# Dynamic convolution and a squared-ReLU feed-forward network: one PSUM tile per output half, first loads in float32, first softmax rows moved within SBUF, conv tiles at multiples of 8

## The chip, the cores and the metric

The kernel runs on one core of one Trainium2 chip. Its time is the device time of one launch in microseconds; the median of several runs is compared. One further execution is taken by the hardware profiler: its own time and its trace are what the rows below come from.

## The reference

Two stages follow one another. First a causal convolution whose weights are given per position: for each of 8 x 4096 positions and 8 heads, a softmax over 7 taps weights the position and the six before it, per head of 24 channels (192 channels in all). Then a feed-forward network without biases, 192 to 2048 to 192, with a squared ReLU between.

```python
w = np.exp(weight_gen - max); w = w / (w.sum(-1) + 1e-9)      # [8, 4096, 8, 7]
x_unf = x_pad[:, idx, :].reshape(B, S, K, H, 24)              # the 7 rows that end at s
a = np.einsum('bshk,bskhg->bshg', w, x_unf).reshape(-1, 192)  # dynamic convolution
h = np.maximum(a @ w_in, 0.0)                                 # 192 -> 2048
out = (h * h) @ w_out                                         # 2048 -> 192, float32
```

## The kernel before

The 32768 positions are cut into 64 blocks of 512 (`TB`), 8 to a batch entry. Products run in float16 with float32 sums. The instructions of each engine run in the order in which the program writes them, and each of the queues (SP's and GpSimd's DMA issues among them) is in order too: what waits at its head holds what stands behind it. The framework puts in the waits between engines, by tile: a writer of a tile waits for its readers and the other way round; a buffer of a pool is given out again when the last user of its tile is done.

Softmax. `Softmax` (L118) handles a stretch of rows: `load` (L123) brings the raw weights from DRAM by SP's queue, `exp` (L146) runs on ScalarE, `recip` (L158) and `scale` (L167) on VectorE, and the result goes to a tile `v` with r rows to a partition, in a layout with zero padding between taps. `store` (L185) writes it to a DRAM buffer `vd`. The first batch entry is cut into three parts of 8, 8 and 16 rows to a partition (`FIRST`, tiles `v_first`); each later one is one part of 32, which `plan` (L413) spreads over some of the blocks ahead of it.

Convolution. A block is covered by 5 overlapping tiles of 128 input rows (`starts`, step `STEP`), which yield the output ranges between `bounds`. `x_load` (L221) brings the x rows by GpSimd's queue and casts float32 to float16 on the way; `wr_load` (L225) brings the softmax rows from `vd` by SP's queue. `st_band` (L231) multiplies them with a band mask on VectorE and so makes a banded matrix `bd` for each tile; its slice of the mask begins at `shifts`. `st_conv` (L272) multiplies x with the bands in 72 matmuls of 32 or fewer output columns, in which a piece of the lower and one of the upper 256 positions run side by side in the array; `conv_pieces` (L252) pairs them. `st_y_evac` (L290) copies the result to SBUF as float16 `y`.

Feed-forward. `st_mm1` (L297) computes 2 of 16 chunks of the hidden layer into a PSUM tile `h`; lower and upper positions use the two halves of the array's rows, so `w_i` holds w_in twice, in partitions 0 to 63 and 64 to 127. `st_relu` (L331) runs on ScalarE into `t1` (pool `p_t1`), `st_sq` (L336) on VectorE into `g`. `st_mm2` (L313) adds the chunks up in `o`, one tile of two PSUM banks, half 0 of the positions in one and half 1 in the other. `o_copy` (L342) copies a half to SBUF on ScalarE, `o_store` writes it out. The three buffers of `ps_h` serve `h` and the conv's result `yp`; `ps_o` has one buffer.

The loop (L430). Block j runs conv(j+1) and the copy of its y, bands 0 to 2 of block j+2, the first product for four pairs of chunks (`G0`) with relu and square, then the second product of block j-1 for the chunks `G1`: half 0, its copy, half 1, its copy, and the store. Then bands, a part of a softmax, the first product for `G1` and the second product of block j for `G0`. At the end `wr_load(j+3)`. Blocks 0 and 2 are `late`: their bands come at the end. For j = 0 conv(1) stands in the middle of the block.

The start (L368 to L410). 48 matmuls on zeros warm TensorE up. x of block 0, w_in (four quarters) and w_out go by GpSimd's queue with the cast; w_in is copied to the upper partitions by SP's queue. The first two softmax parts are computed and stored to `vd`, and `wr_load(0)` and `wr_load(1)` read them from there. Then come the bands, the conv and the copy of y of block 0.

Of the kernel before, what the change touches and what calls it, by code (L numbers as in the profile page):

```python
# [9 lines left out]
def kernel(  # L10
# [47 lines left out]
    STEP = 98  # L58
    BASE = -8
    starts = [BASE + STEP * i for i in range(NT)]  # L60
    bounds = [0, 104, 208, 304, 400, TB]
# [7 lines left out]
    p_wg = ctx.enter_context(tc.tile_pool(name="p_wg", bufs=2))  # L69
    p_sm = ctx.enter_context(tc.tile_pool(name="p_sm", bufs=2))  # L70
# [4 lines left out]
    p_t1 = ctx.enter_context(tc.tile_pool(name="p_t1", bufs=6))  # L75
# [25 lines left out]

    WQ = 4

    def load_w_in():
        src = moe_w_in.rearrange("(k p) f -> p k f", p=RT)
        for q in range(WQ):
            c = slice(q * Dff // WQ, (q + 1) * Dff // WQ)
            nc.gpsimd.dma_start(out=w_i[0:RT, :, c], in_=src[:, :, c])

    def copy_w_in(q):  # L110
        c = slice(q * Dff // WQ, (q + 1) * Dff // WQ)
        nc.sync.dma_start(out=w_i[RT:P, :, c], in_=w_i[0:RT, :, c])

    def load_w_out():
        nc.gpsimd.dma_start(out=w_o, in_=moe_w_out.rearrange("(c p) m -> p c m", p=P))


    class Softmax:  # L118
# [27 lines left out]
        def exp(self, lo, hi):  # L146

            if lo == 0:
                self.ex = p_wg.tile([P, self.rh, HP, KK, 2], f32, name=f"ex{self.r}")
                self.ssum = p_sm.tile([P, self.rh, HP, 2], f32, name=f"ssum{self.r}")  # L150
                self.rcp = p_sm.tile([P, self.rh, HP, 2], f32, name=f"rcp{self.r}")
            nc.scalar.activation(  # L152
                out=self.ex[:, lo:hi].rearrange("p r g k e -> p (r g) k e"),
                in_=self.wg[:, lo:hi].rearrange("p r (g e) k -> p (r g) k e", e=2),
                func=ActF.Exp,
            )
# [67 lines left out]

    def wr_load(j):  # L225
        wr_t[j] = p_wr.tile([P, NT, HP, SL * 2], f16, name="wr")
        block_load(
            j, wr_t[j].rearrange("p t g c -> p t (g c)"), vd_t[j // NBB], H * SL, nc.sync
        )

# [82 lines left out]
    def st_mm2(j, fps, halves=(0, 1)):  # L313

        if fps[0] == 0:
            o_t[j] = ps_o.tile([P, 2, TB], f32, name="o")
        o = o_t[j]
        for fp in fps:
            for jj in range(2):
                fc = 2 * fp + jj  # L320
                for half in halves:
                    for cc in range(2):
                        nc.tensor.matmul(  # L323
                            out=o[:, half, cc * Dm : (cc + 1) * Dm],
                            lhsT=g_t[(j, fp)][:, half, jj, cc * P : (cc + 1) * P],
                            rhs=w_o[:, fc, :],
                            start=(fc == 0 and cc == 0), stop=(fc == NF - 1),
                            skip_group_check=True,
                        )
# [12 lines left out]
    def o_copy(j, half, copy):  # L342
        if half == 0:
            o_sb_t[j] = p_os.tile([P, 2, 2 * Dm], f32, name="o_sb")
        copy(out=o_sb_t[j][:, half], in_=o_t[j][:, half, 0 : 2 * Dm])  # L345
# [20 lines left out]
    with nc.allow_low_precision("fp16 matmul pipeline"), tc.manual_schedule():  # L366
# [7 lines left out]
        for i in (0, 1):  # L374
            parts[i].load(nc.sync)
            nc.vector.memset(v_first[i], 0.0)

        wp = ps_h.tile([P, 2 * TB], f32, name="wp", tag="h")
        for i in range(48):
            nc.tensor.matmul(  # L380
                out=wp[:, 0:TB], lhsT=warm[:, 0:P], rhs=warm, start=True, stop=True
            )
        x_load(0)
        load_w_in()
        band_mask()

        for i in (0, 1):
            s = parts[i]
            s.exp(0, s.rh)
            s.recip(0, s.rh)  # L390
            s.scale(0, s.rh, nc.vector)
            s.store(nc.sync)
            if i == 0:
                wr_load(0)
                wr_load(1)
                copy_w_in(0)
                copy_w_in(1)
        copy_w_in(2)
        copy_w_in(3)
        parts[2].load(nc.sync)  # L400
        x_load(1)
        load_w_out()
# [4 lines left out]
        nc.gpsimd.memset(v_first[2], 0.0)  # L407
        nc.gpsimd.memset(v_big, 0.0)
        x_load(2)
        wr_load(2)  # L410
# [19 lines left out]
        for j in range(NBLK):  # L430
# [9 lines left out]
            late = j in (0, 2)  # L440
            if j:
                if j + 1 < NBLK:
                    st_conv_alloc(j + 1)
                    st_conv(j + 1)
                    st_y_evac(j + 1)
                if not late:
                    st_bands(j + 2, BANDS[0:3])
            else:
                st_bands(1, BANDS[0:3])
# [9 lines left out]
            elif NBLK > 1:  # L459
                st_bands(1, BANDS[3:5])  # L460
                st_conv_alloc(1)
                st_conv(1)
                st_y_evac(1)
            if not late:
                st_bands(j + 2, BANDS[3:5])
            if hi:
                s = rows_of[nb]
                s.exp(lo, hi)
                s.recip(lo, hi)
                s.scale(lo, hi, nc.vector)  # L470
# [6 lines left out]
            st_mm2(j, G0)  # L477
            if late:
                st_bands(j + 2, BANDS)
# [38 lines left out]
```

## Time and profile before

| | us |
|---|---|
| median of 3 runs (865.69 to 867.62) | 865.83 |
| profiled execution | 863.74 |
| its span, from the first to the last instruction | 862.0 |
| TensorE, ScalarE, VectorE, GpSimd busy | 789.4, 604.4, 592.2, 69.4 |

The profile names the engines PE (TensorE), PEld (its weight loads), DVE (VectorE), ACT (ScalarE), POOL (GpSimd) and SP (the engine that only issues DMAs); SPq and POOLq are DMA issues. A line of the timeline gives the start, the busy time and the operation with its output and inputs, and in brackets how long the engine was idle before it and what ended that. The granted clock is a share of 2.4 GHz: 1.00 is that level and 0.50 is 1.2 GHz.

### The profile page before, as it was taken

The page shows a single profiled execution, that of the slowest core. Times are in us where ns is not written, and L with a number is a line of the kernel's source. Part 1 is how long each engine was busy: PE and PEld are TensorE (multiplying, and loading weights), DVE is VectorE, ACT ScalarE, POOL GpSimd, SP SyncE. Part 2 cuts the span into 40 slices and gives each one's busy share as a digit, 9 for nine tenths or more (in the row PEclk, how much of TensorE's full clock was granted, in tenths as well). Part 3 has the DMA queues.
Part 4 walks back from the last instruction along what each step waited for, and adds up shares of the span by engine and source line. Part 5 has one row for each costly group of instructions (what it writes and reads, how often), then busy time and mean ns, then how long its engine had stood idle before and what let it go on. Part 6 is the DMA issues. An engine that isn't in the chain of part 4 may idle for free.

```text
span 862.0 us, 32753 instructions
## 1 busy us (share of the span) xinstructions
PE 789.4 (92%) x14896; PEld 682.2 (79%) x14896; DVE 592.2 (69%) x1159; ACT 604.4 (70%) x753; POOL 69.4 (8%) x86
## 2 busy tenths in 40 slices
PE   6898999999999999999999999999999999999997
PEld 3577788888888888888888888888888888878886
DVE  5668777776776767777677767767767766656643
ACT  1575777777777767767767767777677677677674
POOL 6100000000001000010000000000000000000000
PEclk9799999999999999999999999999999999999999
DMA  9632532335433443335333353333533234232111
GB/s 182 143 77 40 142 49 59 69 47 134 69 47 60 88 103 59 68 48 136 66 47 62 66 122 64 63 48 68 134 53 65 58 58 83 58 64 42 46 39 37
DMA packets 124906, 63.85 MB, mean 74 GB/s; under 512 B 87777, under 2 KB 122464, under 8 KB 124000
## 3 DMA queue, kind: packets, MB, share of 16 engines
q0 software_dynamic: 45008, 17.31, 18.6%
q1 hardware_dynamic: 79488, 44.26, 18.3%
q8 instruction: 116, 1.90, 0.9%
q10 hardware_dynamic: 272, 0.20, 0.1%
q14 instruction: 22, 0.18, 0.1%
HBM read 48.90 MB, written 29.36 MB: 91 GB/s over the span
## 4 chain that ended last, share of the span: by engine, by line
PE 62%; issue 16%; ACT 16%; DVE 3%; DMA 2%; ACTq 0%; SPq 0%; DVEq 0%
PE o L323 31%; PE h L304 26%; ACT t L334 12%; PE yp L280 6%; ACT o_sb L345 3%; DVE bd L239 1%; DMA wr<-vd 1%; DVE g L340 1%; DMA vd<-v_first 1%; ACT ex L152 0%; DVE ssum L160 0%; DVE v_first L173 0%; DVE rcp L165 0%; DMA wg<-in_weight_gen_dram 0%; DVE v_big L173 0%
## 5 line engine op out<-in xcount | busy, mean ns | idle before, releaser
L334 ACT ACTIVATE t<-h 128x1024 f16<-128x1024 f32 x512 | 483.0, 1029 | 10.0 <-PE h L304 9.5
L340 DVE TENSOR_TENSOR g<-t 128x1024 f16<-128x1024 f16 x512 | 346.2, 690 | 190.4 <-ACT t L334 190.1
L323 PE MATMUL o<-w_o,g 128*128 128x192 f16 x4096 | 370.3, 246 | 53.8 <-ACT o_sb L345 53.8
L323 PEld LDWEIGHTS <-g 128*128 128x128 f16 x4096 | 332.3, 98 | 90.0 <-issue 71.9
L304 PE MATMUL h<-y,w_i 64*128 64x256 f16 x6144 | 364.6, 271 | 1.4 <-ACT y L293 0.9
L304 PEld LDWEIGHTS <-w_i 64*128 64x128 f16 x6144 | 292.9, 95 | 53.2 <-issue 11.5
L239 DVE TENSOR_TENSOR bd<-wr,mask 128x832 f16<-128x832 f16 (+2 forms) x320 | 168.7, 579 | 10.1 <-DMA wr<-vd 10.0
L293 ACT CAST y<-yp 128x768 f16<-128x768 f32 x64 | 51.1, 799 | 137.6 <-PE yp L280 137.6
L345 ACT COPY o_sb<-o 128x384 f32<-128x384 f32 x127 | 62.8, 494 | 101.0 <-PE o L323 101.0
L219 POOL DMA_DIRECT2D xt<-in_x_dram x56 | 48.3, 862 | 621.6 <-PE yp L280 596.3
L280 PE MATMUL yp<-bd,xt 128*32 128x104 f16 (+14 forms) x4608 | 63.8, 203 | 12.2 <-DVE bd L239 11.8
L280 PEld LDWEIGHTS <-xt 128*32 128x32 f16 (+3 forms) x4608 | 52.1, 91 | 24.5 <-issue 24.5
L160 DVE TENSOR_REDUCE ssum<-ex 128x64 f32<-128x448 f32 (+6 forms) x49 | 25.9, 530 | 57.7 <-ACT ex L152 57.7
L173 DVE TENSOR_TENSOR v_big<-ex,rcp 128x112 f16<-128x112 f32 (+3 forms) x192 | 32.8, 235 | 1.6
L152 ACT ACTIVATE ex<-wg 128x448 f32<-128x448 f32 (+6 forms) x49 | 26.4, 539 | 2.6 <-DMA wg<-in_weight_gen_dram 2.6
L165 DVE RECIPROCAL rcp<-ssum 128x64 f32<-128x64 f32 (+6 forms) x49 | 23.3, 476 | 1.7
L380 PE MATMUL wp<-warm 128*128 128x512 f16 x48 | 12.0, 417 | 1.3 <-DVE warm L373 1.3
L211 POOL DMA_DIRECT2D xt<-in_x_dram x8 | 4.6, 573 | 88.8 <-PE yp L280 88.0
L380 PEld LDWEIGHTS <-warm 128*128 128x128 f16 x48 | 5.0, 106 | 7.8 <-issue 1.9
L173 DVE TENSOR_TENSOR v_first<-ex,rcp 128x112 f16<-128x112 f32 (+2 forms) x32 | 6.3, 269 | 0.2
L217 POOL DMA_DIRECT2D xt<-in_x_dram x8 | 6.0, 749 | 0.5 <-issue 0.5
L345 DVE COPY o_sb<-o 128x384 f32<-128x384 f32 x1 | 0.6, 559 | 3.6 <-PE o L323 3.6
(14 smaller groups left out, 14.1 us busy)
## 6 DMA issues: line engine op xcount, KB each, us to landing
out_dram<-o_sb SPq DMA_DIRECT2D x63, 384.0 KB, 2.7
xt<-in_x_dram POOLq DMA_DIRECT2D x56, 240.0 KB, 4.1
wg<-in_weight_gen_dram SPq DMA_DIRECT2D x6, 1064.0 KB, 6.7
wr<-vd SPq DMA_DIRECT2D x56, 80.0 KB, 2.9
vd<-v_big SPq DMA_DIRECT2D x7, 512.0 KB, 2.9
xt<-in_x_dram POOLq DMA_DIRECT2D x8, 192.0 KB, 3.8
wg<-in_weight_gen_dram SPq DMA_DIRECT2D x1, 896.0 KB, 5.3
wg<-in_weight_gen_dram SPq DMA_DIRECT2D x2, 392.0 KB, 3.2
```

The lines of the kernel that those rows point to most:

```text
L152: nc.scalar.activation(out=self.ex[:, lo:hi].rearrange("p r g k e -> p (r g) k e"), in_=self.wg[:, lo:hi].rearrange("p r (g e) k -> p (r g ...
L160: nc.vector.tensor_reduce(out=ssum.rearrange("p r g e -> p (r g) e"), in_=self.ex[:, lo:hi].rearrange("p r g k e -> p (r g) e k"), axis=Ax ...
L173: eng.tensor_tensor(out=bass.AP(tensor=v.tensor, offset=v.offset + lo * H * SL + lo % SL * 2 + g * SL * 2, ap=[list(v.ap[0]), [H * SL + 2, ...
L219: eng.dma_start(out=dst, in_=rows(src, t0 + BASE, width))
L239: nc.vector.tensor_tensor(out=bd_t[j][:, H * lo : H * hi].rearrange("p (g m c) -> p g m c", g=HP, c=2 * SL), in0=wr_t[j][:, i].unsqueeze(2 ...
L280: nc.tensor.matmul(out=yp_t[j][p0 : p0 + m, col + a : col + b], lhsT=x_t[j][:, i, 32 * q : 32 * q + m], rhs=bd[:, h // 2, h % 2, a - lo : ...
L293: nc.scalar.copy(out=y, in_=yp_t[j][:, 0 : NK * TH].rearrange("p (k c) -> p k c", k=NK))
L304: nc.tensor.matmul(out=h[:, half, jj, :], lhsT=w_i[r0 : r0 + RT, k, fc * P : (fc + 1) * P], rhs=y_t[j][r0 : r0 + RT, k, :], start=(jj == 0 ...
L323: nc.tensor.matmul(out=o[:, half, cc * Dm : (cc + 1) * Dm], lhsT=g_t[(j, fp)][:, half, jj, cc * P : (cc + 1) * P], rhs=w_o[:, fc, :], star ...
L334: nc.scalar.activation(out=t1, in_=h_t[(j, fp)], func=ActF.Relu)
L340: nc.vector.tensor_tensor(out=g, in0=t1, in1=t1, op=AluOp.mult)
L345: copy(out=o_sb_t[j][:, half], in_=o_t[j][:, half, 0 : 2 * Dm])
```

## The change

The output tile `o` becomes two tiles, `o0` and `o1`, one for each half. The start loads x of blocks 0 and 1, w_in and w_out as float32 by SP's queue into staging tiles (pool `p_st`, two buffers of each kind; w_in is loaded twice, once for each half of the partitions), and ScalarE (x, two quarters of w_in) or GpSimd (the other two quarters, w_out) casts them. The softmax rows of blocks 0 and 1 are moved from `v_first[0]` to `wr` within SBUF, five DMAs a block, and the stores to `vd` stand later in SP's queue. For these moves tile starts have to be multiples of 8, so the step of the conv tiles becomes 104, their base -32, and two of the bounds move. `p_t1` has 5 buffers instead of 6, `ex` its own pool. In block 0 the bands of block 1 stand ahead of the loop, those of block 2 in its middle, and its part of the softmax moves to the end. There are 52 warm-up matmuls.

```diff
-    STEP = 98
-    BASE = -8
+    STEP = 104
+    BASE = -32
-    bounds = [0, 104, 208, 304, 400, TB]
+    bounds = [0, 96, 200, 304, 400, TB]
...
+    p_ex = ctx.enter_context(tc.tile_pool(name="p_ex", bufs=2))
+    p_st = ctx.enter_context(tc.tile_pool(name="p_st", bufs=2))
-    p_t1 = ctx.enter_context(tc.tile_pool(name="p_t1", bufs=6))
+    p_t1 = ctx.enter_context(tc.tile_pool(name="p_t1", bufs=5))
...
-    def load_w_in():
+    def load_w_in(q):
         src = moe_w_in.rearrange("(k p) f -> p k f", p=RT)
-        for q in range(WQ):
-            c = slice(q * Dff // WQ, (q + 1) * Dff // WQ)
-            nc.gpsimd.dma_start(out=w_i[0:RT, :, c], in_=src[:, :, c])
-
-    def copy_w_in(q):
         c = slice(q * Dff // WQ, (q + 1) * Dff // WQ)
-        nc.sync.dma_start(out=w_i[RT:P, :, c], in_=w_i[0:RT, :, c])
-
-    def load_w_out():
-        nc.gpsimd.dma_start(out=w_o, in_=moe_w_out.rearrange("(c p) m -> p c m", p=P))
+        w_st[q] = p_st.tile([P, NK, Dff // WQ], f32, name="w_st")
+        for r0 in (0, RT):
+            nc.sync.dma_start(out=w_st[q][r0 : r0 + RT], in_=src[:, :, c])
+
+    def cast_w_in(q, copy):
+        c = slice(q * Dff // WQ, (q + 1) * Dff // WQ)
+        copy(out=w_i[:, :, c], in_=w_st[q])
+
+    def load_w_out(q):
+        n = NF // WO
+        wo_st[q] = p_st.tile([P, n, Dm], f32, name="wo_st")
+        nc.sync.dma_start(
+            out=wo_st[q],
+            in_=moe_w_out[q * n * P : (q + 1) * n * P].rearrange("(c p) m -> p c m", p=P),
+        )
+
+    def cast_w_out(q, copy):
+        n = NF // WO
+        copy(out=w_o[:, q * n : (q + 1) * n], in_=wo_st[q])
...
+    def x_load_f32(j):
+        x_st[j] = p_st.tile([P, NT, D], f32, name="x_st")
+        block_load(j, x_st[j], x[j // NBB], D, nc.sync)
+
+    def x_cast(j, copy):
+        x_t[j] = p_x.tile([P, NT, D], f16, name="xt")
+        copy(out=x_t[j], in_=x_st[j])
...
+    def wr_load_sbuf(j, s):
+
+        wr_t[j] = p_wr.tile([P, NT, HP, SL * 2], f16, name="wr")
+        for i in range(NT):
+            t0 = j * TB + (0 if i == 0 and j == 0 else starts[i]) - s.t0
+            nc.sync.dma_start(
+                out=wr_t[j][:, i].rearrange("p g c -> p (g c)"),
+                in_=s.v[t0 // s.r : (t0 + P) // s.r, HALO : HALO + s.r].rearrange(
+                    "p r g c e -> p r (g c e)"
+                ),
+            )
...
-            o_t[j] = ps_o.tile([P, 2, TB], f32, name="o")
+            o_t[j] = [ps_o.tile([P, TB], f32, name=f"o{half}") for half in range(2)]
...
-                            out=o[:, half, cc * Dm : (cc + 1) * Dm],
+                            out=o[half][:, cc * Dm : (cc + 1) * Dm],
...
-        copy(out=o_sb_t[j][:, half], in_=o_t[j][:, half, 0 : 2 * Dm])
+        copy(out=o_sb_t[j][:, half], in_=o_t[j][half][:, 0 : 2 * Dm])
...
-        for i in range(48):
+        for i in range(52):
...
-        x_load(0)
-        load_w_in()
         band_mask()
...
+        nc.gpsimd.memset(v_first[2], 0.0)
+        nc.gpsimd.memset(v_big, 0.0)
+        vec, act, pool = nc.vector.tensor_copy, nc.scalar.copy, nc.gpsimd.tensor_copy
...
+        parts[0].load(nc.sync)
+        x_load_f32(0)
+        parts[1].load(nc.sync)
+        load_w_in(0)
+        load_w_in(1)
+        s0, s1 = parts[:2]
+        s0.exp(0, s0.rh)
+        s1.exp(0, s1.rh)
+        s0.recip(0, s0.rh)
+        s0.scale(0, s0.rh, nc.vector)
+        wr_load_sbuf(0, s0)
+        x_cast(0, act)
+        x_load_f32(1)
+        cast_w_in(0, act)
+        cast_w_in(1, act)
+        load_w_in(2)
+        s1.recip(0, s1.rh)
+        s1.scale(0, s1.rh, nc.vector)
+        wr_load_sbuf(1, s0)
+        load_w_in(3)
+        for q in range(WO):
+            load_w_out(q)
+            if q == 0:
+                s0.store(nc.sync)
+                s1.store(nc.sync)
+                wr_load(2)
+                for i in (2, 3):
+                    cast_w_in(i, pool)
+            cast_w_out(q, pool)
         parts[2].load(nc.sync)
-        x_load(1)
-        load_w_out()
         st_bands(0, BANDS)
         st_conv_alloc(0)
         st_conv(0)
         st_y_evac(0)
-        nc.gpsimd.memset(v_first[2], 0.0)
-        nc.gpsimd.memset(v_big, 0.0)
+        x_cast(1, act)
+        st_bands(1, BANDS)
         x_load(2)
-        wr_load(2)
...
-            late = j in (0, 2)
+            late = j == 2
...
-            else:
-                st_bands(1, BANDS[0:3])
...
-                st_bands(1, BANDS[3:5])
                 st_conv_alloc(1)
                 st_conv(1)
                 st_y_evac(1)
+                st_bands(2, BANDS[0:3])
...
-            if hi:
+            if hi and j:
...
             st_mm2(j, G0)
+            if hi and not j:
+                softmax(rows_of[nb], lo, hi)
```

## Rows read from the trace of the kernel before

**Rows 1.** Page, part 1: busy us, share of the span, instructions of each engine.

```profile
PE 789.4 (92%) x14896; PEld 682.2 (79%) x14896; DVE 592.2 (69%) x1159; ACT 604.4 (70%) x753; POOL 69.4 (8%) x86
```

**Rows 2.** List of waits: engine line <- releaser, total us, times, longest us.

```profile
PE o L323 <- ACT o_sb L345: 53.8, 64, 0.8
```

**Rows 3.** Timeline of block 20: start, busy us, engine, line, operation, [idle before].

```profile
290.11 0.94 PE L280 MATMUL yp<-bd,xt 128*32 128x104 f16 x72
...
290.98 2.79 PE L304 MATMUL h<-y,w_i 64*128 64x256 f16 x48
...
293.71 1.49 PE L323 MATMUL o<-w_o,g 128*128 128x192 f16 x16
...
296.05 1.48 PE L323 MATMUL o<-w_o,g 128*128 128x192 f16 x16 [0.84 <-ACT o_sb L345]
...
297.46 2.79 PE L304 MATMUL h<-y,w_i 64*128 64x256 f16 x48
297.56 0.48 ACT L345 COPY o_sb<-o 128x384 f32<-128x384 f32 x1 [1.57 <-PE o L323]
...
298.28 0.27 DVE L160 TENSOR_REDUCE ssum<-ex 128x16 f32<-128x112 f32 x1 [0.93 <-ACT ex L152]
...
300.19 2.81 PE L323 MATMUL o<-w_o,g 128*128 128x192 f16 x32
...
302.93 0.94 PE L280 MATMUL yp<-bd,xt 128*32 128x104 f16 x72
```

**Rows 4.** Timeline of block 2, the one with 16 softmax rows.

```profile
62.65 3.76 ACT L334 ACTIVATE t<-h 128x1024 f16<-128x1024 f32 x4
...
63.72 0.83 PE L304 MATMUL h<-y,w_i 64*128 64x256 f16 x12 [0.35 <-ACT t L334]
...
66.45 2.49 DVE L340 TENSOR_TENSOR g<-t 128x1024 f16<-128x1024 f16 x4
```

**Rows 5.** Timeline of the tail.

```profile
856.58 1.48 PE L323 MATMUL o<-w_o,g 128*128 128x192 f16 x16 [0.57 <-ACT o_sb L345]
```

**Rows 6.** Timeline of the start.

```profile
5.61 2.61 POOL L97 TENSOR_SCALAR_AFFINE_SELECT mask<-mask 128x256 f16<-128x256 f16 x2
...
6.86 2.23 DVE L173 TENSOR_TENSOR v_first<-ex,rcp 128x112 f16<-128x112 f32 x8
...
10.89 1.46 DVE L173 TENSOR_TENSOR v_first<-ex,rcp 128x112 f16<-128x112 f32 x8
11.79 2.47 POOL L408 MEMSET v_big<- 128x2816 f16 x1
...
22.74 5.63 PE L304 MATMUL h<-y,w_i 64*128 64x256 f16 x48 [0.89 <-ACT y L293]
...
41.73 2.79 PE L304 MATMUL h<-y,w_i 64*128 64x256 f16 x48
```

**Rows 7.** Chain of work that ended last, 0 to 60 us: start, us, what.

```profile
9.11 4.75 DMA vd<-v_first
...
13.88 4.51 DMA wr<-vd
```

**Rows 8.** Windows: stretch, us, busy of each engine, granted clock, DMA share, GB/s.

```profile
17.00:19.00 2.00, 0.00 (x0) 0.00 (x0) 0.51 (x2) 0.00 (x0) 0.00 (x0) 0.75 1.62 193
19.00:21.00 2.00, 1.48 (x50) 1.11 (x50) 2.00 (x5) 0.00 (x0) 0.00 (x0) 0.50 1.53 235
...
300.00:301.00 1.00, 1.00 (x16) 0.82 (x11) 0.77 (x2) 1.00 (x2) 0.00 (x0) 1.00 1.08 385
```

**Rows 9.** Page, part 6: DMA issues, count, KB each, median us to landing.

```profile
xt<-in_x_dram POOLq DMA_DIRECT2D x56, 240.0 KB, 4.1
...
wr<-vd SPq DMA_DIRECT2D x56, 80.0 KB, 2.9
...
wg<-in_weight_gen_dram SPq DMA_DIRECT2D x2, 392.0 KB, 3.2
```

**Rows 10.** DMA queues view, issues: count, KB each, median us to landing.

```profile
vd<-v_first SPq DMA_DIRECT2D x1, 256.0 KB, 2.0
```

## What the change does to the time, predicted from these rows

> **What bounds the kernel now.** I read the page's busy times first, then the list of waits, then one block of the main loop line by line, then the two ends of the span. TensorE is busy 92% of the span, ScalarE 70%, VectorE 69% [rows 1]: TensorE is the engine to look at, so the question is what stands in its remaining 8%. The list of waits answers it: of TensorE's idle time 53.8 us, in 64 pieces of at most 0.8 us, is its second product waiting for ScalarE's copy of the output [rows 2]. The block shows where. The block's conv starts at 290.11, the next one's at 302.93, so a block is 12.82 us. Inside, TensorE runs without a hole except at one place: the 16 matmuls of output half 0 start at 293.71 and take 1.49 us, and the 16 matmuls of half 1 start only at 296.05, behind an idle time of 0.84 us that ended with that copy [rows 3]. Half 1 needs nothing of that copy; both halves are parts of one tile `o`, and the wait is on the tile.
>
> **Change 1, an output tile per half.** The same work without the wait stands in the same block: the other 32 matmuls of the second product start at 300.19 and are done at 302.93, 2.74 us; those of the halves take from 293.71 to 297.46, 3.75 us [rows 3]. The difference, 1.01 us, is the wait plus the emptying and refilling of the pipeline around it; the idle time alone would be 53.8 / 64 = 0.84. I take 1.01, since it compares start with start, and keep 0.84 as the poor end. 63 blocks give 63 x 1.01 = 63.6 us. In the tail half 1 starts at 856.58, after 0.57 us of the same wait [rows 5]: 0.6 us more. Together 64.2 us (53.8 at the poor end).
>
> What is late next? After the change half 1 starts at once and everything behind it moves up by 1.0 us. ScalarE waits 1.57 us for half 1 before it copies it, which becomes 0.57: it still waits for TensorE and not TensorE for it. VectorE's row sum of the softmax waits 0.93 us for the exponential [rows 3]; that goes to about zero and VectorE stays on time. Loads per block are 604.4 / 64 = 9.4 us for ScalarE and 592.2 / 64 = 9.3 us for VectorE [rows 1], against a new block of 11.81 us, so neither becomes the bound. The accumulator's next use, the first half of the second product at 300.19, comes 2 us after the copies even when all move up together, so the two new tiles with one buffer each cost no wait. They take the same two banks.
>
> **Change 2, `p_t1` with 5 buffers in place of 6.** It would cost something where ScalarE runs five relus ahead of VectorE's squares. The worst place is the block with 16 softmax rows: four relus start from 62.65 and the first of their squares at 66.45 [rows 4], so four are open. Five hold them: nothing, and a slip of one more relu would still only shift ScalarE. `p_ex` renames a pool: nothing.
>
> **Change 3, conv tiles.** The widths of the band tiles are the same set (96, 96, 104, 104, 112), so VectorE pays the same. On TensorE the pieces of the two halves run side by side: the longer of each pair were 104, 104, 112 columns (320), now 96, 104, 112 (312). The conv's 0.87 us (290.11 to 290.98) [rows 3] would shrink by 8/320, 0.02 us, or 1.4 us over 64 blocks; if it is bound by issuing 72 instructions, nothing. I take 0.7.
>
> **Change 4, the start.** I count to the first matmul of block 1's first product, at 41.73 us, from which the kernel runs evenly; block 0's starts at 22.74 [rows 6]. Before it stands a detour through DRAM: the store of the first softmax rows takes 4.75 us and their reload 4.51 [rows 7]. Now five moves within SBUF replace both. None is in the trace; bounds are the 2.9 us of a steady `wr` load [rows 9] and that 4.51. With five issues of about 0.45 us behind one another the tile is complete some 4.5 to 6 us after the rows, in place of 9.3, if the queue is free. It isn't quite: SP now carries two softmax loads, x and two quarters of w_in, 2.9 MB, before the moves. At the 385 GB/s that the queues reached in the steady part [rows 8] it is done at about 9.2 us, level with the rows; at two thirds of that at 13. Block 0's first product then starts at 17.5 to 20 us, a gain of 3 to 5 us.
>
> But that is not what block 1 starts on. `x_load(2)` stays on GpSimd's queue, and GpSimd now first casts two quarters of w_in and four of w_out, 2 x 1536 + 4 x 768 = 6144 elements of a partition; before, nothing but memsets and the mask stood there. conv(2) opens block 1 and needs that x. The chain, each step from a row or a neighbour of it: SP has issued the two stores at about 17.5; they land 2.0 us later as the third store did [rows 10], or 4.75 as the first [rows 7]; `wr_load(2)` waits for them, and `load_w_out(1)` stands behind it, issued at about 22; 3 us to land, as the 392 KB loads (3.2) [rows 9], and 1 us to cast (26); `load_w_out(3)` may use the staging buffer only then: 3 us and 1 us (30.5); x in 4.1 us [rows 9] (34.6); conv and the copy of y, 0.9 + 0.8. Block 1's first product starts at about 36.5 to 37: 4.8 us earlier than 41.73.
>
> From that the clock takes something back. With no matmul to run since the warm-up, TensorE's granted clock fell from 2.4 to 1.2 GHz (0.75 as the mean of 17 to 19 us, 0.50 after) [rows 8], and the first product of block 0 then took 5.63 us, against 2.79 us in block 1 [rows 6]. By the chain TensorE is idle from about 29 to 34.6, so block 1 opens slowly: 2.8 us lost. Net 2 us gained. The four extra warm-up matmuls end about 1 us later than before, ahead of the bands: nothing.
>
> Bounds: with stores that land in 2 us and no fall of the clock the gain is 8 us. The casts have no row; GpSimd's nearest are the memset, 2816 elements in 2.47 us (0.88 ns each), and the mask's select, two of 256 elements in 2.61 us (5.1 ns each) [rows 6]. A cast is a plain stream like the memset, with a read added: I take 1.3 ns, 8 us in all, mostly under the loads. At 5.1 ns it is 31 us, and from about 16 us on they would hold x until 51: a loss of 11 + 2.8 = 14 us. ScalarE's casts lie ahead of conv(0) and are covered by the wait for the moves.
>
> Sum: 862.0 - 64.2 - 0.7 - 2.0 = 795.1 us of span. The profiled execution took 863.74, 1.74 more than its span, and the median of the runs is 865.83, another 2.09 more: 798.9, rounded to 799.
>
> **Rivals.**
> (a) GpSimd's casts are slow. Eight scalings with two operands took 2.23 us while GpSimd ran the select, and 1.46 us while it only wrote a memset [rows 6]; so the two engines do hold each other up. The casts read, and VectorE's bands, squares and scalings have two operands: some 9.3 us of them in a block [rows 1], all of which may delay the casts in front of x, to 808. Slower casts give up to 815.6. The Trainium skill, "SBUF — State Buffer", section "Who interferes with whom", says that a VectorE instruction with two SBUF inputs contends with a GpSimd instruction that reads SBUF and not with one that only writes; the 2.23 against 1.46 us agrees.
> (b) Another wait takes the place of the one removed. One is in sight: where the exponential is long, the fourth tile of the next product waited 0.35 us for ScalarE's relu [rows 4]. That chain starts at the copy of half 1 and moves with it, which speaks against it. If each block paid it, 22 us come back: 821.
> (c) The split doesn't remove the wait, because the order and not the shared tile makes it. Against it: half 1's operands were ready and the release is the copy's. 862.0 - 0.7 - 2.0 + 3.83 = 863.1, no change.
> (d) Slower than before: the casts on GpSimd hold x(2) and w_out for so long that the start eats all 66.9 us. Each ns per element costs 6.1 us, so it decides from 1.3 + 11 = 12 ns on, at twice the slowest row; 18 ns would give 900.
>
> **Chances.** The forecast 0.72; (a) 0.16; (b) 0.06; (c) 0.04; (d) 0.02. The forecast's own ends are 862.0 - 64.2 - 1.4 - 8 + 3.83 = 792.2 and, with 0.84 us per block, 809.3; (a) reaches 815.6. I say 790 to 815. A difference of 0.3% is about what a measurement of this kernel can tell: faster 0.94, same 0.04, slower 0.02.
>
> **What would show it.** Right: no wait of the second product for `o_sb` in the list, a block of 11.8 us from conv to conv, ScalarE's wait before the copy of half 1 down to about 0.6 us, block 1's first product at 36 to 37 us, TensorE idle before conv(2) with x as the releaser. Wrong: a new idle time of TensorE inside the block, a conv(2) that waits for something else, casts on GpSimd of more than 2 ns per element, or a clock that falls outside the start.

## The result, and the profile after

The kernel takes 806.39 us after the change (median of 4 runs, 803.74 to 810.45) and 865.76 us before, beside it on the same chip: a ratio of 0.932, with a 95% interval of 0.9274 to 0.936. The profiled execution took 806.78 us with a span of 804.9. The forecast was 799.0, in a range of 790 to 815. The main loop gained what was forecast; the start lost where a gain was forecast.

The page of the changed kernel, part 1, answers to [rows 1]:

```profile
PE 779.5 (97%) x14900; PEld 682.0 (85%) x14900; DVE 592.9 (74%) x1159; ACT 609.8 (76%) x757; POOL 70.3 (9%) x84
```

TensorE's busy time is down by 9.9 us, 9.5 of them in the second product (370.3 to 360.8 us); the rest of the 57.1 us of span was idle time. Its list of waits answers to [rows 2] (engine line <- releaser: total us, times, longest):

```profile
PE yp L315 <- DMA xt<-in_x_dram: 8.7, 1, 8.7
PE yp L315 <- DVE bd L274: 6.1, 6, 2.9
PE o L358 <- POOL w_o L130: 2.4, 1, 2.4
PE h L339 <- POOL w_i L118: 1.5, 1, 1.5
...
PE h L339 <- ACT t L369: 0.3, 1, 0.3
```

The 53.8 us for `o_sb` are gone, and no wait that recurs in every block has come. What is left stands at the start, with one new wait of 8.7 us for an x. The timeline of one block, which answers to [rows 3] (start, busy us, engine, line, operation):

```profile
255.32 0.92 PE L315 MATMUL yp<-bd,xt 128*32 128x96 f16 x72
256.17 2.79 PE L339 MATMUL h<-y,w_i 64*128 64x256 f16 x48
258.89 2.81 PE L358 MATMUL o<-w_o,g 128*128 128x192 f16 x32
261.64 2.79 PE L339 MATMUL h<-y,w_i 64*128 64x256 f16 x48
264.37 2.81 PE L358 MATMUL o<-w_o,g 128*128 128x192 f16 x32
267.11 0.68 PE L315 MATMUL yp<-bd,xt 128*32 128x96 f16 x48
...
261.74 0.48 ACT L380 COPY o_sb<-o 128x384 f32<-128x384 f32 x1 [0.56 <-PE o L358]
```

The two halves are one group of 32 matmuls without a hole, and from conv to conv a block is 267.11 - 255.32 = 11.79 us. ScalarE still waits for half 1, 0.56 us in place of 1.57. The tail answers to [rows 5] in the same way:

```profile
795.68 5.45 PE L358 MATMUL o<-w_o,g 128*128 128x192 f16 x64
```

One row on each side divides the time: block 2's first product, of before and then of after.

```profile
54.75 1.48 PE L304 MATMUL h<-y,w_i 64*128 64x256 f16 x24
```

```profile
60.26 1.48 PE L339 MATMUL h<-y,w_i 64*128 64x256 f16 x24
```

From there to the end of the span it is 862.0 - 54.75 = 807.3 us before and 804.9 - 60.26 = 744.6 after: 62.6 us gained. Up to there 5.5 us are lost. The lost time is in these rows of the start, timeline first, then the chain of waits (start, us, what):

```profile
17.38 0.22 PE L315 MATMUL yp<-bd,xt 128*32 128x96 f16 x2 [2.88 <-DVE bd L274]
...
21.02 4.97 PE L339 MATMUL h<-y,w_i 64*128 64x256 f16 x48 [0.89 <-ACT y L328]
...
45.77 1.48 PE L315 MATMUL yp<-bd,xt 128*32 128x96 f16 x72 [8.73 <-DMA xt<-in_x_dram]
47.18 3.86 PE L339 MATMUL h<-y,w_i 64*128 64x256 f16 x48
...
8.56 4.12 SPq L259 DMA_DIRECT2D wr<-v_first  x5
```

```profile
4.83 11.64 DMA w_st<-in_moe_w_in_dram
...
17.15 4.89 DMA wr<-v_first
...
23.79 5.78 DMA vd<-v_first
...
30.05 3.75 DMA wo_st<-in_moe_w_out_dram
...
39.17 6.56 DMA xt<-in_x_dram
```

Block 1's first product comes at 47.18, where it came at 41.73 before [rows 6]: the x of conv(2) was asked for at 39.17 and landed at 45.73, and TensorE stood idle for 8.73 us. The same links as in the forecast's chain are there, in the same order; each is later, and each transfer takes longer.

### The profile page after: what moved, and what is told of

It reads as the page before. It is cut to its first block, busy times and chain, and to the rows that moved or that the text cites. A ratio compares the mean times of both kernels' runs of the same rounds, so it can differ in the third digit from the quotient of the medians.

```text
span 804.9 us, 32787 instructions
## 1 busy us (share of the span) xinstructions
PE 779.5 (97%) x14900; PEld 682.0 (85%) x14900; DVE 592.9 (74%) x1159; ACT 609.8 (76%) x757; POOL 70.3 (9%) x84
## 4 chain that ended last, share of the span: by engine, by line
PE 92%; DMA 4%; DVE 1%; SPq 1%; issue 1%; POOL 0%; ACT 0%; DVEq 0%; POOLq 0%
PE o L358 43%; PE h L339 43%; PE yp L315 7%; DMA w_st<-in_moe_w_in_dram 1%; DMA xt<-in_x_dram 1%; DMA vd<-v_first 1%; DMA wr<-v_first 1%; DVE bd L274 1%; DMA wo_st<-in_moe_w_out_dram 0%; POOL w_o L130 0%; SPq L114 0%; DVE g L375 0%; DVE v_big L188 0%; ACT ex L167 0%; DVE ssum L175 0%
## 5 line engine op out<-in xcount | busy, mean ns | idle before, releaser
L358 PE MATMUL o<-w_o,g 128*128 128x192 f16 x4096 | 360.8, 247 | 2.4 <-POOL w_o L130 2.4
L274 DVE TENSOR_TENSOR bd<-wr,mask 128x768 f16<-128x768 f16 (+2 forms) x320 | 170.0, 583 | 12.5 <-DMA wr<-vd 7.6
L234 POOL DMA_DIRECT2D xt<-in_x_dram x55 | 47.5, 864 | 554.0 <-PE yp L315 519.4
L315 PE MATMUL yp<-bd,xt 128*32 128x96 f16 (+17 forms) x4608 | 61.7, 203 | 15.1 <-DMA xt<-in_x_dram 8.7
L226 POOL DMA_DIRECT2D xt<-in_x_dram x7 | 3.9, 559 | 80.9 <-PE yp L315 80.9
L232 POOL DMA_DIRECT2D xt<-in_x_dram x7 | 5.2, 748 | 0.0
L118 ACT CAST w_i<-w_st 128x1536 f16<-128x1536 f32 x2 | 2.9, 1472 | 2.9 <-DMA w_st<-in_moe_w_in_dram 2.9
```

Source lines behind the costliest of these rows:

```text
L234: eng.dma_start(out=dst, in_=rows(src, t0 + BASE, width))
L274: nc.vector.tensor_tensor(out=bd_t[j][:, H * lo : H * hi].rearrange("p (g m c) -> p g m c", g=HP, c=2 * SL), in0=wr_t[j][:, i].unsqueeze(2 ...
L315: nc.tensor.matmul(out=yp_t[j][p0 : p0 + m, col + a : col + b], lhsT=x_t[j][:, i, 32 * q : 32 * q + m], rhs=bd[:, h // 2, h % 2, a - lo : ...
L358: nc.tensor.matmul(out=o[half][:, cc * Dm : (cc + 1) * Dm], lhsT=g_t[(j, fp)][:, half, jj, cc * P : (cc + 1) * P], rhs=w_o[:, fc, :], star ...
```

## The experiments

**The split alone, and the change without it.** Two kernels divide the change: before with nothing but a tile per half (e1), and after with one tile `o` again (e2).

```diff
-            o_t[j] = ps_o.tile([P, 2, TB], f32, name="o")
+            o_t[j] = [ps_o.tile([P, TB], f32, name=f"o{half}") for half in range(2)]
...
-        copy(out=o_sb_t[j][:, half], in_=o_t[j][:, half, 0 : 2 * Dm])
+        copy(out=o_sb_t[j][:, half], in_=o_t[j][half][:, 0 : 2 * Dm])
```

> The kernel before with one edit: an output tile per half; loads, softmax moves and conv tiles stay as they were. Theory: the wait for the shared tile is worth 1.0 us in each of 63 blocks and 0.6 in the tail, 64 us, and the changed start gave some 5 of them back. Then this kernel is faster than the changed one: 865.8 - 64 = 802 us, block 1's first product still at 41.7 us, the block 11.8 us. Rival 1: the start is neutral and the split is worth only the 59 us that were measured: 806. Rival 2: the shorter block hangs on the conv tiles too: block over 11.9 us and 810 or more.

Measured: 802.59 us, ratio 0.9277 (0.926 to 0.9295).

> The changed kernel with one edit undone: one output tile for both halves again. Theory: everything else in the change costs 5 us at the start and gains 1 us in the conv; with the wait back the block is 12.8 us and the time 806.4 + 64 = 870, slower than the kernel before by 4 to 5 us, with block 1's first product at 47 us. Rival: the rest of the change is neutral or gains, and the time is 866 or less.

Measured: 869.76 us, ratio 1.005 (1.0032 to 1.0068). The list of waits of e2 has the old row again:

```profile
PE o L358 <- ACT o_sb L380: 53.3, 64, 0.8
```

So the split is worth 62 to 63 us, all of the gain and more; the rest of the change costs 4 to 5 us, whichever way it is taken.

**Is it the shared tile, or the copy between the halves?** e3 keeps one tile and moves the order: both halves' matmuls first, then both copies.

```diff
             for half in (0, 1):
                 st_mm2(j - 1, G1, (half,))
+            for half in (0, 1):
                 o_copy(j - 1, half, nc.scalar.copy)
```

> The kernel before with one edit: both halves of the second product first, then both copies; still one output tile. Theory: half 1 waits because the tile has a reader between its writers; with the readers behind both, TensorE's wait for the copy goes as with two tiles (64 us), but ScalarE now has two copies to make before its first relu of the next product, 0.4 to 0.5 us later than with the split, so the fourth tile of that product waits for the relu 0.1 us in blocks without softmax and 0.4 us in blocks with: 802 + 0.3 x 63 = 815 to 825 us, new waits of TensorE for the relu in nearly each block. Rival: ScalarE's delay is hidden and it is as fast as the split, 802. Rival 2: the wait isn't the tile's, and 0.84 us of idle time stays in front of half 1: 866.

Measured: 817.03 us, ratio 0.9439 (0.9417 to 0.9462). TensorE's and the weight loads' waits of e3, then the weight loads' of e1:

```profile
PE h L304 <- ACT t L334: 7.5, 22, 0.7
...
PEld L304 <- issue: 28.3, 114, 0.9
```

```profile
PEld L304 <- issue: 12.3, 71, 0.6
```

The 53.8 us go away here too, so the wait hung on a copy standing between two groups of matmuls on one tile. But ScalarE now does both copies after the second half, its relus start later, and TensorE waits for them in the blocks that carry a part of a softmax: these take 11.98 to 12.30 us from conv to conv in e3's steady part and 11.82 to 11.92 in e1's, the blocks without one 11.82 in both. 14 us come back. The two tiles remove the wait and leave ScalarE its early start.

**What the start waits for.** e4 changes one place of the changed kernel: x of block 2 is asked for behind GpSimd's two casts of w_in, ahead of those of w_out.

```diff
                 for i in (2, 3):
                     cast_w_in(i, pool)
+                x_load(2)
...
         x_cast(1, act)
         st_bands(1, BANDS)
-        x_load(2)
```

> The changed kernel with one move: GpSimd loads x of block 2 behind its two casts of w_in, ahead of the four casts of w_out. Theory: conv(2) waited 8.7 us for this x; without that it is ready when the second product of block 0 ends, and what is late next is the third softmax load, which holds ScalarE's queue until about 40 us: block 1's first product at 41 to 42 us in place of 47.2, TensorE still idle in front of it and its clock down: 806.4 - 5.5 = 801. Rival: x comes no earlier, as the DMA queues are full with the weights until then, and the time stays at 806.

Measured: 800.31 us, ratio 0.9249 (0.9234 to 0.9264), 6 us under the changed kernel: the place of `x_load(2)` behind the casts was the last link. What is late next in e4, by its chain of waits:

```profile
21.99 5.98 DMA vd<-v_first
...
28.45 5.97 DMA wo_st<-in_moe_w_out_dram
...
36.28 4.58 DMA wg<-in_weight_gen_dram
```

conv(2) runs at 38.54, and then its y waits behind an exponential on ScalarE whose weights landed at 40.9: the same queue of SyncE, one link further. Block 2's first product is at 53.42.

Three kernels ask what holds that queue. e5 reorders it, puts two w_out loads and a w_g load on ScalarE's queue, and issues the ten moves of softmax rows one behind the other. e8 moves only block 0's rows within SBUF and sends block 1's through DRAM; it also issues the first two w_out loads and the third softmax load earlier, as e5 does, but on SyncE's queue. e9 sends all of them through DRAM, as before the change. The cores of the three edits, each against e4, in this order:

```diff
         wr_load_sbuf(0, s0)
         x_cast(0, act)
-        x_load_f32(1)
...
-        load_w_in(2)
...
         wr_load_sbuf(1, s0)
+        s0.store(nc.sync)
+        x_load_f32(1)
+        load_w_in(2)
+        s1.store(nc.sync)
...
+        load_w_out(0, nc.scalar)
+        load_w_out(1, nc.scalar)
+        parts[2].load(nc.scalar)
```

```diff
         wr_load_sbuf(0, s0)
+        s0.store(nc.sync)
+        x_load_f32(1)
...
-        wr_load_sbuf(1, s0)
+        s1.store(nc.sync)
+        wr_load(1)
```

```diff
-        wr_load_sbuf(0, s0)
+        s0.store(nc.sync)
+        wr_load(0)
...
-        wr_load_sbuf(1, s0)
+        wr_load(1)
```

> The kernel of e4 with the queues reordered and nothing else: the moves of block 1 stand right behind those of block 0 on SP's queue, the store of the first softmax rows ahead of the third quarter of w_in and that of the second ahead of the fourth, and the first two quarters of w_out and the third softmax load are issued by ScalarE's queue behind its casts of w_in, so that they wait neither for the stores nor for a cast. Theory: in e4 the start is a chain of waits at the head of SP's queue (stores 6 us, then w_out 6 us, then the softmax load 4.6 us); in parallel they end by about 31 us, the waits of TensorE for the w_out cast (4.7 us) and of ScalarE for the softmax load (10 us) go, and the first product of block 2 starts at 46 to 48 us in place of 53.4: 800.3 - 6 = 794. Rival: the DMA engines are full in the start, and the same bytes in another order end no earlier: 799 or more.

Measured: 799.04 us, ratio 0.9239 (0.9225 to 0.9253). The expectation missed by 5 us. The time is the rival's, but its reason isn't shown: between 12 and 16 us the DMA engines moved only 113 GB/s. SyncE's queue in e5, then its waits ahead of these moves (total us, times, longest), then the issues of the ten moves in the changed kernel (ns, shortest, median and longest):

```profile
8.26 9.73 SPq L259 DMA_DIRECT2D wr<-v_first  x10
```

```profile
SPq L259 <- DMA w_st<-in_moe_w_in_dram: 2.0, 2, 1.2
SPq L259 <- DMA wr<-v_first: 1.5, 1, 1.5
```

```profile
L259 SPq DMA_DIRECT2D wr<-v_first x10: 544/597/619, 8.6 to 19.7; - x10
```

The ten moves stretch over 9.73 us of the queue, but one issue takes 0.54 to 0.62 us, in e5 as in the changed kernel; 3.5 us are waits between the issues, which ended with the landing of a w_in load or of an earlier move. Nothing in the program makes a move wait for w_in; why the queue stood there is open. Nor do the moves alone account for the low rate: e9, which has none, moved 109 GB/s from 12 to 16 us. What stands behind the ten moves comes late: x of block 1 is asked for at 18.67, in e4 at 11.69, and conv(1) runs at 30.81 in place of 22.80.

> As e4 (x of block 2 asked for early), but only block 0's softmax rows are moved SBUF to SBUF; block 1's go through DRAM, the store before w_in's third load, the read back behind it, and the two casts of w_out and w_g stay behind. It takes half of the moves off SyncE's queue (each was 0.6 to 0.97 us there). Theory A, SyncE's queue of small moves is what holds block 2's data and weights back: block 2's first product comes at 43 to 46 us in place of 53.4, and the time falls to 790 to 794 us. Theory B, the bytes that the start must bring (or the engines behind the DMAs) hold it: block 2's first product stays at 51 to 54 us, and the time is 799 to 802 us.

Measured: 798.64 us, ratio 0.9214 (0.918 to 0.9248), but one execution of four took 792.7 and the others 798.4 to 799.2. The profiled one is the 792.7: block 2's first product at 47.07, between the two theories' values, and no fall of the granted clock in the start. The median is at theory B's edge. The two numbers answer to two different courses of the start, see below. Since e8 changes the order of the loads too, its time isn't the price of the five moves alone.

> As e4, but all softmax rows of the start go through DRAM again, as in the kernel before; the split, the float32 loads and the casts stay. It prices the moves. If the moves are worth what the detour cost the first block (9.3 us of store and read back against about 6 us of moves): block 0's first conv 2 to 3 us later than in e4, and the time 802 to 804 us. If their issue on SyncE's queue (10 moves, 6 to 10 us) costs the later loads as much as they save: 798 to 801 us, with block 2's data landing earlier than in e4.

Measured: 801.93 us, ratio 0.9278 (0.9257 to 0.9298). Against e4's 800.31 the ten moves are worth 1.6 us, with intervals that overlap; the first conv is at 17.67 in e9 and 15.30 in e4. The detour through DRAM costs the first block 2.4 us at most (the changed kernel, with the same moves as e4, has its first conv at 17.38), and the blocks behind it get most of that back.

**Wider loads.** e6 (from e4) and e7 (from e5) load each quarter of w_in, with its copy on the other 64 partitions, by three DMAs over 128 partitions whose source has a first dimension of size 2 and step 0.

```diff
-        for r0 in (0, RT):
-            nc.sync.dma_start(out=w_st[q][r0 : r0 + RT], in_=src[:, :, c])
+        for k in range(NK):
+            nc.sync.dma_start(
+                out=w_st[q][:, k],
+                in_=bass.AP(
...
+                    ap=[[0, 2], [Dff, RT], [1, Dff // WQ]],
```

> The kernel of e4 with one edit: each quarter of w_in is loaded by three DMAs over all 128 partitions (one for each 64 rows of w_in, read twice) in place of two over 64 partitions each; the same bytes in the same runs of 2 KB. Theory: the second quarter landed at 14.4 us, and 2.9 MB had then moved since 1.7 us, 225 GB/s in place of the 385 that I had counted with, because a DMA over 64 partitions is slower than one over 128; with 128 the quarters land some 3 us earlier, and so does the rest of the chain behind them: 797. Rival: two DMAs in flight, one for each half, already fill the engines, and one more issue per quarter costs 0.6 us of SP's time: 800 to 802.

> The edits of e5 and of e6 together. Theory: they add, as the one shortens waits at the queue's head and the other the transfers: 794 - 2 = 792. Rival: the transfers are not what ends last once the queues are free, and it is as e5 within 1 us.

Measured: 844.72 and 844.68 us, ratio 0.9764 for both (0.9748 to 0.978): some 45 us slower than the kernels that they came from. One window of e6 (stretch; busy us of PE, PEld, DVE, ACT, POOL; granted clock, DMA share, GB/s):

```profile
16.00:20.00 4.00, 0.00 (x0) 0.00 (x0) 0.00 (x0) 0.00 (x0) 0.00 (x0) 1.00 0.13 51
```

A DMA share of 0.13 is 2 of 16 engines. The Trainium skill, "DMA: Bandwidth & Descriptors", section "Why a DMA increments its semaphore by 16 and not by 1", says that a DMA is spread over the largest number of engines, up to 16, that divides the slowest dimensions of both sides; with a size of 2 that is 2, and the row agrees. Whether 128 partitions would load faster than twice 64 stays open.

**Why e8 had two times.** My theory was TensorE's clock: in e8's profiled execution it stayed at 1.00, since the warm-up ended just ahead of the first conv. e10 and e11 make the warm-up longer.

```diff
-        for i in range(52):
+        for i in range(60):
```

> e8 with 60 warm-up matmuls in place of 52. The profiled execution of e8 took 792.7 us with a granted clock that stayed at 1.00 through the start, its three others 798.4 to 799.2; the warm-up of the first ended at 15.4 us, half a microsecond before its first conv, where the other kernels' ended at 14 to 15. Theory: the 6 us between the executions are the clock alone, which falls where TensorE stands idle between warm-up and first conv. Then with 8 more matmuls the time is 791 to 795 us in all executions, and the clock of every one 0.996 or more. Rival: the executions differ in their transfers. Then the median stays at 797 to 800 us.

Measured: 800.43 us (800.17 to 800.79), ratio 0.9248 (0.9234 to 0.9261). The theory fell: the first product ran at the full clock (2.80 us), and the time was 7.7 us above e8's profiled execution. The trace shows another cause. GpSimd's second cast of w_in and VectorE's work at that moment, in e8 and then in e10:

```profile
27.50 1.47 POOL L118 CAST w_i<-w_st 128x1536 f16<-128x1536 f32 x1 [3.48 <-DMA w_st<-in_moe_w_in_dram]
...
26.97 5.09 DVE L375 TENSOR_TENSOR g<-t 128x1024 f16<-128x1024 f16 x3
29.90 1.60 POOL L130 CAST w_o<-wo_st 128x768 f16<-128x768 f32 x2
```

```profile
27.47 6.52 POOL L118 CAST w_i<-w_st 128x1536 f16<-128x1536 f32 x1 [3.32 <-DMA w_st<-in_moe_w_in_dram]
...
27.10 1.88 DVE L375 TENSOR_TENSOR g<-t 128x1024 f16<-128x1024 f16 x3
28.90 2.55 DVE L274 TENSOR_TENSOR bd<-wr,mask 128x768 f16<-128x768 f16 x5
31.38 1.28 DVE L375 TENSOR_TENSOR g<-t 128x1024 f16<-128x1024 f16 x2
```

The cast starts at the same time in both, to 0.03 us. In e8 GpSimd goes through in 1.47 us, and VectorE's three squares take 5.09 where three take 1.88: the second takes 1.95 us beside this cast, the third 2.62 beside the two casts of w_out. In e10 VectorE runs its squares and bands without a gap until 32.66, and the cast ends at 33.99, 1.33 us behind them, about what a cast takes by itself. One of the two engines stands still. What decides which isn't shown: in both runs the cast begins while a square is under way.

The cast's end then sets the time. It comes 5.0 us later in e10 (33.99 against 28.97), the product that needs it starts 5.0 us later (34.05 against 29.03), and block 2's first product 6.6 us later (53.64 against 47.07). The other 1.6 us come with the granted clock, which falls to 0.50 in that wait: the two products behind it take 2.74 and 4.12 us in place of 1.48 and 2.80, 2.6 us more, of which e8 loses a part to short waits of its own there (0.28 us for w_out, 0.42 for x). But e10's clock had fallen once before, ahead of the cast (stretch, us, granted clock, DMA share, GB/s):

```profile
24.00:26.00 2.00, 0.95 1.08 194
26.00:28.00 2.00, 0.50 1.12 263
28.00:30.00 2.00, 0.70 1.01 364
30.00:32.00 2.00, 1.00 0.08 32
32.00:34.00 2.00, 0.65 0.00 0
34.00:36.00 2.00, 0.50 0.19 16
```

In e8 it is 1.00 in all of these windows, though TensorE was idle ahead of conv(1) for about as long (2.53 us, in e10 2.59). The first fall slows a product at 27.30 to 2.39 us and costs nothing by itself, as TensorE has to wait until 34.05 anyway. Whether it has a part in which engine stands still, no run tells; in e11, whose cast was slow too, the clock had fallen there as well (0.66 as the mean of 24 to 28 us). The Trainium skill, "SBUF — State Buffer", section "Who interferes with whom", says that a VectorE instruction with two SBUF inputs contends with a GpSimd instruction that reads SBUF, and that the order of issue decides who is blocked. Both traces agree with the first. The second doesn't follow the starts in the trace: the nine VectorE instructions that ran while e10's cast stood still all began behind it, and e8's last square began at 29.43, ahead of w_out's casts at 29.90, and ended behind them, at 32.05. That e8's three other executions went as e10's did is inferred from their time; they have no trace.

> e8 with 68 warm-up matmuls in place of 52, so that they end at 17.5 to 19 us, behind the first bands: the first conv comes 1.5 to 3 us later than in e8. By the theory of the clock: 792 to 796 us in all executions, about 1 to 2 us above e10 where e10 holds the clock, and below it where 60 do not. By the rival (transfers): 798 to 802 us.

Measured: 796.89 us (793.63 to 801.26), ratio 0.9194 (0.9171 to 0.9217), the lowest median of all, though its executions overlap with those of e5 and e8. The profiled execution is the slowest of its four, 801.26, and its cast of w_in took 6.79 us; the fastest is 793.63. By its numbers alone this run decides nothing: its median lies between the two expectations. In the three traces of e8, e10 and e11 the cast's course and the time go together.

> The changed kernel with 68 warm-up matmuls in place of 52. There the first conv came 2.9 us behind the warm-up and the first product ran at the half clock, 4.97 us; but block 1 opens with a conv whose x landed at 45.7 us, after TensorE had stood idle for 8.7 us. If x sets the start, the first product falls to 2.8 to 3.1 us and nothing is gained: 805 to 808 us, x landing at 45 to 46 us, and the clock falls before block 1 as it did. If the chain through TensorE sets it (relus, casts, the next loads), 2 to 3 us come off: 802 to 804 us.

Measured: 805.24 us, ratio 0.9305 (0.9291 to 0.9319), with these rows:

```profile
20.80 2.80 PE L339 MATMUL h<-y,w_i 64*128 64x256 f16 x48 [0.89 <-ACT y L328]
...
44.84 1.47 PE L315 MATMUL yp<-bd,xt 128*32 128x96 f16 x72 [8.08 <-DMA xt<-in_x_dram]
```

Block 0's product lost its 2.2 us of half clock, and conv(2) still waited for x until 44.8: the cold first block costs the changed kernel nothing, because x sets the start. A clock that is kept early didn't help here, with TensorE idle for 8 us later on: the product behind conv(2) took 4.26 us.

## Why the prediction was right, and where it was not

**The split** (forecast 64.2 us, poor end 53.8): right, in mechanism and nearly in size. The block is 11.79 us, forecast 11.81. e1 from its block 2's first product (55.35) to its end (801.2) takes 745.9 us against 807.3: 61.4 us over 62 blocks and the tail, where the forecast's rate gives 62 x 1.01 + 0.6 = 63.2. Taking start against start, and not the idle time of 0.84, was the right choice: e2's row shows 53.3 us of idle time, but its absence is worth 62 to 63.

The 1.8 us that are missing stand in one block. From conv to conv e1 is 1.00 to 1.02 us shorter than the kernel before in every block from block 2 on, but for block 3, which is 0.63 us longer. There the first product, of before and then of after, is this:

```profile
71.88 2.79 PE L304 MATMUL h<-y,w_i 64*128 64x256 f16 x48
```

```profile
76.39 4.46 PE L339 MATMUL h<-y,w_i 64*128 64x256 f16 x48
```

The granted clock had fallen to 0.50 behind an idle time of 2.3 us in which conv(4) waited for its bands; e1's product took 4.42. Before the change the same idle time, 2.30 us, left the clock at 1.00, and so it did in e12, where the product took 2.79 and the block 13.58 us, 0.97 under the 14.55 of before. So the split gives its 1.0 us there too, and a fall of the clock took 1.6 of it; why the clock falls there in some executions and not in others isn't shown. The prediction had let the clock fall in the start alone.

**The covers named for it** held. ScalarE's wait before half 1's copy went to 0.56 us (forecast 0.57), no wait for relu recurs, and `p_t1` with 5 buffers shows in no wait of ScalarE for the squares.

**Conv tiles** (forecast 0.7 us, 0 to 1.4): the conv takes 256.17 - 255.32 = 0.85 in place of 0.87 us, and the main part of the changed kernel is 745.9 - 744.6 = 1.2 us shorter than e1's, which has the old tiles. The steady blocks say the same: 11.80 and 11.90 us where e1's are 11.82 and 11.92. In the upper half of the bounds: it follows the columns.

**The start** (forecast 2.0 us gained, between 14 lost and 8 gained): wrong in sign, inside the bounds. Measured at block 2's first product it is 5.5 us later, and the one block ahead of it that the split shortened had given about 1.0: some 6.5 lost. The chain was the right one; these terms of it were mis-sized:
- The moves: 0.45 us of issue each were assumed; an issue took 0.54 to 0.62, and with a wait of 1.0 us among them, which ended with a w_in landing, the five took 4.12 us of the queue. The bands of block 0 began at 16.77, 8.2 us after the first issue at 8.56; 4.5 to 6 had been forecast. Block 0's first product came at 21.02, later than the forecast's 17.5 to 20.
- The stores' issue: forecast 17.5, measured 23.2. I had priced the loads ahead of them at 385 GB/s, the rate of a steady stretch [rows 8]; the start reached 224 to 245 GB/s between 4 and 12 us, and a w_in load was 11.64 us in landing. From the first move at 8.56 to the stores the queue took 14.6 us: about 10.3 for 16 issues, and 4.3 of waits, which ended with landings of w_in, ScalarE's cast of it or ScalarE's copy of y.
- The stores' landing: 5.78 us, against 2 to 4.75.
- w_out's loads and casts after that: the last cast ended at 39.2 (38.40 + 0.83), forecast 30.5; x landed 6.56 us after its issue, not 4.1, with a w_g load of 1064 KB under way that had been issued 2.8 us ahead of it. x was there at 45.73, forecast 34.6.
- The cold clock: 2.8 us taken; the slow conv (1.48 against 0.92) and product (3.86 against 2.79) cost 1.6.

The chain was 11 us too short by x's landing. x alone held block 1 (8.73 us of idle time), but e4 shows the next link close behind it: with x early, conv(2) still comes at 38.54, 7.2 us sooner. All these prices came from the steady part or from a start with fewer loads on SyncE's queue; here six loads (x, w_g and four of w_in, issued from 1.7 to 5.7 us) are under way together before the first move is issued.

**From span to median**: I added 2.09 us because the profiled execution of before lay that far under its median. After, it lay 0.39 above. That sum was a property of one execution, and 2.5 us of the forecast's number rested on it. The errors add up: 799.0 + 8.5 (start) + 1.8 (split, 1.6 of it the clock in block 3) - 0.5 (conv) - 2.5 = 806.3. That the 2.5 us go the other way is luck: in span alone the forecast was 795.1 and the measurement 804.9, 9.8 us off.

**The rivals.** (a) Slow casts on GpSimd: as priced, no. A cast of 1536 elements took 1.46 us, 0.95 ns an element, faster than the 1.3 assumed, and VectorE paid instead (five bands in 3.78 us, not 2.57). But its mechanism is real: in e10 and e11 the cast takes 6.5 and 6.8 us. (b) No new wait in the block. (c) and (d) fell.

**What would show it**: no wait for `o_sb`, the 11.8 us block, the 0.6 us of ScalarE and x as the releaser before conv(2) all came as written. "Block 1's first product at 36 to 37" didn't, and it was the sign that told where to look. Of the signs of being wrong one came, a clock that falls outside the start: in block 3, for 1.6 us.

## What to carry to other kernels

A wait of TensorE for a copy, between two groups of matmuls that write different parts of one tile, was worth its start against start, nearly a fifth more than the idle time that the list shows, and a tile for each part gave it back, with slack in the engines behind. A start must not be priced with the rates and landings of the steady part: list every DMA in flight at that moment, count an issue for each transfer, small or large, let each staged buffer's release hold the whole queue, and put the load that the next block opens with ahead of what is staged. The best of these kernels (e11, 796.89 us) is 9.5 us below the changed one by another order of the same loads and casts, five moves replaced by a read back from DRAM, and 16 warm-up matmuls more.

## What the runs showed of the hardware

- The issue of one move of 16 KB within SBUF takes SyncE's queue 0.54 to 0.62 us, that of a w_in load of 384 KB 0.60 to 0.73 (in e8). Splitting a transfer into five was about five times the issue. While loads are under way the queue also stood still between issues that need nothing of them, 3.5 us among e5's ten moves.
- GpSimd's cast from float32 to float16 takes 0.95 ns per element of a partition undisturbed. Beside VectorE's two-operand instructions either can stop the other: a VectorE band took 1.73 us in the changed kernel in place of some 0.5 (five take 2.57), a GpSimd cast 6.5 to 6.8 in place of 1.46, and it waited through nine VectorE instructions in a row, all begun behind it.
- A DMA whose source began with a dimension of size 2 ran on 2 of 16 engines at 51 GB/s, a fifth of what the other loads of the start reached.
- The granted clock fell to 0.50 behind a TensorE idle time of 2.3 us ahead of conv(4) in the changed kernel and stayed at 1.00 behind the same idle time in e12's execution: one trace doesn't settle whether a stretch runs at 2.4 or 1.2 GHz.
